# A three-part kernel on one Trainium2 core: score halves and transposes joined into shorter lists, loads and softmax moved ahead, tails' order written out

## The chip, the cores and the metric

The kernel runs on one core of a Trainium2 chip. The metric is the device time of one execution in microseconds; the median of three runs is given. The engines are TensorE (PE; its weight loads are PEld), VectorE (DVE), ScalarE (ACT), GpSimd (POOL) and SyncE (SP), which here issues loads and stores.

## The reference, cut

Three stages in a row, for 4 batches of 576 tokens: an attention over 32 memory slots made from `phi`, a mixture of experts with a sticky choice, and a gated convolution.

```python
a = softmax over seq of phi                       # (4, 8, 576, 32)
k_m, v_m = einsum('bhsm,bhsd->bhmd', a, k), ... v
attn = softmax(q @ k_m.T / sqrt(64)); x = attn @ v_m
logits = x @ w_gate; gate = sigmoid(x @ w_local)
e = argmax(logits[s]) if s == 0 or gate[s] < 0.5 else previous e
x[s] = p[e] * (relu(x[s] @ w1[e]) @ w2[e])
h = relu(x @ w_in); c = conv3(h, conv_w)
out = (h * sigmoid(c)) @ w_out
```

## The kernel before, in words

The work of a batch is two units (pairs of four heads), 2b and 2b+1. For a unit, `load_phi` and `load_kv` fetch it; `psoft` (`phi_softmax`: `phi_max` on VectorE writes `nm`, `phi_exp` on ScalarE writes `ex`, `phi_sums` on VectorE) makes A without its division; `pback` (`phi_back`, line 401) turns A on TensorE with five transposes into a PSUM tile `pa`, which ScalarE copies to `a`; `mem` (`memory`) multiplies A by k and v into `pk`, and its `memory_out` first lets VectorE use `pk` (`q0r`, line 452), then ScalarE scale it into `pm` (line 455). `back` (`memory_back`, line 459) turns both units' `pm` on TensorE into `pkt`, ScalarE copies that to `vt`.

For a batch, `scores` makes two halves of the scores on TensorE (`sc_0`, `sc_1`, a two-bank PSUM tile each, of a pool with two buffers). `strn` (`scores_back`, line 514) turns a half on VectorE into `st`; `smx`, `ssub`, `sexp`, `ssum` are the steps of its softmax (`mx`, `sd`, `smx`, `at`), and `ssoft` in the table at line 966 is all of them with `strn` ahead, through `slot_top` (line 557). `gatew` makes `pw`; `flog` (`first_expert`, line 601) makes the first token's logits `pfc` on TensorE, and their maximum `flm` and MAX_INDEX on VectorE, which writes `e0i`, the batch's expert. SP loads `e0i` and then, in one queue, the expert's weights (`w1`: `wa_0` to `wa_3`, `wb_0`, `wb_1`).

Then come the expert's products: `vw` folds the values into the first weights (`pv` on TensorE, its high part `vh` on ScalarE, its low part `vl` on VectorE). `h` (one of 16 for a batch, two halves of 8) is one `ph` of six matmuls in a single bank of a pool of four that also holds `pw`, `pfc`, `pk`, `pkt` and `py`; ScalarE writes its high part and VectorE its low part. `y` (8 for a batch) is one `py` of 24 matmuls. `nar` narrows the 64-bit words of the last stage's weights beside all this on ScalarE, VectorE and GpSimd.

TensorE runs in the order of a list. `OPENING` is written out, and `order` (lines 60 to 111) writes for each batch b its 24 slots (16 `h`, 8 `y`; batch 0 starts at slot 12) and what follows each: `FIRST` for batch 0, a table of its own for the others, with c = b + 1 and d = b + 2 the batches that are being prepared. VectorE's, ScalarE's and SP's instructions of the list are ordered by a scheduler, except in the opening and where an instruction is pinned (`keep_in_program_order`) or named to come after another (`issue_after`, `behind`, `behind_hidden`).

The last stage (`gated`, line 1048) makes, for f = 0 to 7, 12 matmuls `pi` for a batch's first 512 tokens, and for batch 0 also `pit`, the tails of all batches; ScalarE reads them out (`ht`, `htt`), the convolution and the gate follow, and `product` (line 1141) multiplies the result `g` by `w_out` into `po`, for batch 0 mixed between the `pit` by the scheduler.

Of the kernel before, what the change touches and what calls it, by code (L numbers as in the profile page):

```python
# [36 lines left out]
def units(b):  # L37
# [13 lines left out]


FIRST = {
    12: "gatew.1 scores.1.0 flog.1 w1.1 psoft.4", 13: "ssoft.1.0 psoft.5", 16: "pback.4 scores.1.1 ssoft.1.1", 17: "pback.5",
    19: "nar.2 nload.4", 20: "asplit.1.0 asplit.1.1",
    21: "mem.4 mem.5 vw.1.0 vw.1.1 vw.1.2 vw.1.3 back.2", 22: "w2.1.0 w2.1.1 nar.3 nload.5 conv", 23: "q.2.0 q.2.1 save.0",
}


def order():  # L60


    words = [4]

    def each(c, *parts):
        return [f"{part}.{u}" for u in units(c) for part in parts] if c < B else []

    def of(c, *parts):
        return [f"{part}.{c}" for part in parts] if c < B else []

    def narrow_next():
        i = words[0]
        words[0] += 1
        return [f"nar.{i}"] + [f"nload.{i + 2}"] * (i < 14)

    out = []
    for b in range(B):
        c, d = b + 1, b + 2
        whole = c < B
        after = {i: [] for i in range(24)}  # L80
        if b == 0:
            for i, more in FIRST.items():
                after[i] += more.split()
        else:
            for i, more in {
                1: [f"w2.{b}.2"] * (b == 2) + of(c, "frow", "fexp") + [f"save.{b}"],
                2: [f"w2.{b}.2"] * (b != 2) + of(d, "firstq") + each(d, "phi", "kv"),
                3: of(c, "gatew") + [f"rtok.{b // 2}"] * (b == 1) + [f"{item}.{c}.{hf}" for item in ("scores", "strn") for hf in range(2)] * whole
                   + of(c, "flog"),
                5: [f"smx.{c}.0"] * whole,  # L90
                6: [f"ssub.{c}.0", f"sexp.{c}.0"] * whole,
                7: [f"w2.{b}.3"],
                8: [f"ssum.{c}.0", f"smx.{c}.1", f"ssub.{c}.1", f"sexp.{c}.1", f"ssum.{c}.1"] * whole + each(d, "psoft"),
                9: of(c, "w1"),
                10: each(d, "pback"),
                12: [f"asplit.{c}.0", f"asplit.{c}.1"] * whole,
                21: each(d, "mem") + [f"vw.{c}.{q}" for q in range(4)] * whole + of(d, "back") + ["rtok.1"] * (b == 2),
                22: [f"w2.{c}.0", f"w2.{c}.1"] * whole,
                23: [f"q.{d}.0", f"q.{d}.1"] * (d < B),
            }.items():  # L100
                after[i] += more
            for i in ((), (6, 16, 18, 20, 22), (4, 7, 13, 15, 22, 22), (8, ))[b]:
                after[i] += narrow_next()
            if not whole:
                for i, more in {8: "rall rrows rpp", 9: "rown", 10: "close yload.0 win.0 win.1",
                                19: "ysplit.0", 20: "win.2 win.3"}.items():
                    after[i] += more.split()
        for i in range(0 if b else 12, 24):
            out += [f"h.{b}" if i % 12 < 8 else f"y.{b}"] + after[i]
    assert words[0] == 16  # L110
    return out
# [5 lines left out]
def fused_kernel(tc, q, first, first_q, kv, kv_tail, phi, w1, w2, w_in, conv_w, w_out, out):  # L117
# [3 lines left out]
    with (  # L121
# [116 lines left out]
        def behind(name):  # L238

            return tc.issue_after(issued[name]) if name else contextlib.nullcontext()  # L240

        def needed_behind(b):

            return None if b < 2 else f"wb{b - 2}_3"
# [124 lines left out]
        @contextlib.contextmanager  # L369
        def behind_hidden(wanted):  # L370

            with contextlib.ExitStack() as stack:
                if wanted:
                    stack.enter_context(urgent())
                    stack.enter_context(tc.issue_after(hidden_low[-1]))
                yield

        def phi_max(u):
            nms[u] = ap.tile([128, 1], F32, tag="nm", bufs=2, name=f"nm{u}")
            with behind_hidden(u >= 4):  # L380
                nc.vector.tensor_reduce(nms[u], phs[u], AX.X, ALU.max, negate=True)

        def phi_exp(u):
# [130 lines left out]
        def scores_back(b, hf):  # L514

            sts[b, hf] = work(f"st{b}_{hf}")
            nc.vector.transpose(two(sts[b, hf]), scs.pop((b, hf))[:, :, :HALF])

        def behind_h(b):
            return tc.issue_after(hidden_low[-1]) if b > 1 else contextlib.nullcontext()  # L520

        def slot_max(b, hf):
            mxs[b, hf] = ap.tile([128, 18], F32, tag="mx", bufs=2, name=f"mx{b}_{hf}")
# [30 lines left out]
                cols = slice(32 * hs.start, 32 * hs.stop)  # L554
                nc.vector.transpose(attf[b, hf].rearrange("p g t -> p (g t)")[:, cols], st[:, cols])

        def slot_top(b, hf):
            scores_back(b, hf)
            slot_max(b, hf)
            slot_difference(b, hf)  # L560

        def slot_softmax(b, hf):

            slot_top(b, hf)
            slot_exp(b, hf)
            slot_weights(b, hf)

# [361 lines left out]
        def split_tails(yp, nm):  # L929
            y, p = yp  # L930
            t = state.tile([128, 2, 4, B * TW], F32R, tag="ay", name=f"ts{nm}")
            parts = [t[:, i] for i in range(2)]
            if p is not None:
                nc.vector.tensor_tensor(y, y, p.rearrange("p (o s) -> p o s", o=1).to_broadcast([128, 4, B * TW]), ALU.mult)
            split(*parts, y)
            return parts
# [21 lines left out]
        def gated_w(kc):  # L958
# [4 lines left out]
            "phi": load_phi, "kv": load_kv, "q": load_q,  # L963
            "gates": load_gates, "psoft": phi_softmax, "pback": phi_back,
            "mem": memory, "memf": memory_out, "warm": warm, "back": memory_back,
            "scores": scores, "gatew": gate_weights, "firstq": first_queries, "frow": first_row, "fexp": first_weights, "flog": first_expert, "code": first_code, "ssoft": slot_softmax,
            "pmax": phi_max, "pexp": phi_exp, "prec": phi_sums, "smax": slot_top, "strn": scores_back, "smx": slot_max,
            "ssub": slot_difference, "sexp": slot_exp, "ssum": slot_weights, "ahi": attention_high, "alo": attention_low,
            "rtok": route_tokens, "save": save, "rrows": route_rows, "rall": route_all, "rpp": route_scan, "rown": route_first, "asplit": split_attention,
            "vwe": first_vw, "vwh": first_vw_high, "vwl": first_vw_low, "vw": expert_vw, "w2": expert_w2, "nload": load_words, "nar": narrow, "win": gated_w,  # L970
# [77 lines left out]
        def gated(gp, nm, scaled=False):  # L1048
# [23 lines left out]
            def columns(name, y, store, pin=lambda ins: ins, between=lambda f: None):  # L1072

                yh, yl = y
                n = yh.shape[-1]
                before = None
                for f in range(8):
                    fs = slice(f * 128, (f + 1) * 128)
                    ps = pairs[-1].tile([128, 512], F32, tag="pi", bufs=1 if scaled else 4, name=f"pi{name}_{f}")[:, :n]
                    matmul3([(ps, slice(0, n))],  # L1080
                            [((wi[kc][:, 0, fs], wi[kc][:, 1, fs]), (yh[:, kc, :], yl[:, kc, :])) for kc in range(4)], pin)
                    finish = gate(*before, store) if before else lambda: None
                    ht = lp.tile([128, S], F32, tag="cv", name=f"ht{name}_{f}")[:, :n]
# [23 lines left out]
            for b in range(B):  # L1107
# [17 lines left out]
                    while len(wo) < 4 and f >= WO[len(wo)]:  # L1125
                        wo.append(w2_piece(f"wo{len(wo)}", slow(f"wo.{len(wo)}")))

                columns(f"{nm}{b}", ys, store_main, tc.keep_in_program_order if b == 0 else lambda ins: ins, between)
                if b == 0:
                    tails = split_tails(tails, nm)  # L1130
                    yn = load_y(1, first(1))
                    columns(f"{nm}t", tails, store_tail)
                    for f in range(8):
                        close_main(f)
                if b + 1 < B:
                    ys = y_parts(b + 1)
                    split_y(b + 1, yn, *ys)

                pin = tc.keep_in_program_order if b == B - 1 else lambda ins: ins

                def product(ps, c, fr):
                    for f in fr:
# [5 lines left out]
                                                                    start=f == 0 and i == 0, stop=f == 7 and i == 2)).ins]  # L1148

                chunks = [0, 1, 2] + [4] * (b % 2) + [3]  # L1150
                pss = {c: bank(f"po{b}_{c}") for c in chunks[:3]}
                for c in chunks[:3]:
                    product(pss[c], c, range(0, 6))
                for c in chunks:
                    if c in pss:
                        product(pss[c], c, range(6, 8))
# [96 lines left out]
```

## Time and profile before

| | |
|---|---|
| median of 3 runs | 406.47 us (405.45, 406.47, 406.55) |
| the profiled execution | 405.78 us in all, its span 403.9 us |
| TensorE clock granted | 1.00 over the span |
| busy: DVE, ACT, POOL | 283.4 us (70%), 228.1 us (56%), 65.2 us (16%) |
| busy share of the DMA engines, 40 to 60 us and 60 to 80 us | 0.94, 1.02 |

A timeline row gives when an instruction, or a row of equal ones, started, how long it (or the row) took, the engine, the line, the operation and the count. A matmul's end is modelled, so starts are compared with starts. A row such as `x16` for eight matmuls stands for the two passes of each in full fp32. The share of DMA may go a little over 1 in a short stretch.

### The profile page before, as it was taken

The page shows a single profiled execution, that of the slowest core. Times are in us where ns is not written, and L with a number is a line of the kernel's source. Part 1 is how long each engine was busy: PE and PEld are TensorE (multiplying, and loading weights), DVE is VectorE, ACT ScalarE, POOL GpSimd, SP SyncE. Part 2 cuts the span into 40 slices and gives each one's busy share as a digit, 9 for nine tenths or more (in the row PEclk, how much of TensorE's full clock was granted, in tenths as well). Part 3 has the DMA queues.
Part 4 walks back from the last instruction along what each step waited for, and adds up shares of the span by engine and source line. Part 5 has one row for each costly group of instructions (what it writes and reads, how often), then busy time and mean ns, then how long its engine had stood idle before and what let it go on. Part 6 is the DMA issues. An engine that isn't in the chain of part 4 may idle for free. (4 is left out here: it accounts for less than half of the span.)

```text
span 403.9 us, 7760 instructions
## 1 busy us (share of the span) xinstructions
PE 397.2 (98%) x2969; PEld 344.0 (85%) x2970; DVE 283.4 (70%) x545; ACT 228.1 (56%) x457; POOL 65.2 (16%) x128
## 2 busy tenths in 40 slices
PE   7999999999999999999999999999999999999996
PEld 3469998899989998999988888888888888888884
DVE  3689898897689986696868999489601895069500
ACT  4466575565476357465767758468321882268311
POOL 1000201402112211310100314304100041002200
PEclk9999999999999999999999999999999999999999
DMA  7999989999476959945313033200021000200022
GB/s 274 337 382 407 377 274 393 409 404 368 106 265 211 386 127 409 384 148 181 108 54 109 26 105 104 104 2 2 2 78 52 2 0 0 106 0 0 3 80 57
DMA packets 26525, 69.03 MB, mean 171 GB/s; under 512 B 5904, under 2 KB 6672, under 8 KB 26480
## 3 DMA queue, kind: packets, MB, share of 16 engines
q1 hardware_dynamic: 22896, 56.92, 39.5%
q0 software_dynamic: 3584, 11.54, 7.3%
q8 instruction: 25, 0.41, 0.4%
q14 instruction: 20, 0.16, 0.1%
HBM read 52.12 MB, written 16.33 MB: 169 GB/s over the span
## 5 line engine op out<-in xcount | busy, mean ns | idle before, releaser
L166 PE MATMUL py<-h,wb 128*128 128x288 f32 x768 | 104.5, 295 | 0.0
L166 PEld LDWEIGHTS py<-h,wb 128*128 128x128 f32 x768 | 102.4, 188 | 0.4 <-issue 0.3
L1147 PE MATMUL po<-wo,g 128*128 128x512 f32 x360 | 82.9, 389 | 0.0
L166 PE MATMUL pi<-yh,wi 128*128 128x512 f32 x256 | 79.5, 389 | 0.0
L1147 PEld LDWEIGHTS po<-wo,g 128*128 128x128 f32 x360 | 67.4, 188 | 14.0
L166 PEld LDWEIGHTS pi<-yh,wi 128*128 128x128 f32 x256 | 48.1, 188 | 10.0
L1068 DVE SCALAR_TENSOR_TENSOR ct<-ht,convw,ct 128x510 f32<-128x510 f32 x32 | 23.9, 747 | 45.6 <-ACT ct L1066 45.6
L166 PE MATMUL ph<-att,vh 128*128 128x288 f32 x256 | 52.6, 299 | 0.0
L166 PE MATMUL pi<-yl,wi 128*128 128x512 f32 x128 | 49.8, 389 | 0.0
L166 PEld LDWEIGHTS ph<-att,vh 128*128 128x128 f32 x256 | 40.7, 188 | 2.6 <-issue 0.9
L894 POOL DMA_DIRECT2D ydram<-ys x32 | 17.8, 556 | 146.2 <-ACT ys L893 142.8
L166 PE MATMUL ph<-att,vl 128*128 128x288 f32 x128 | 37.7, 296 | 0.0
L809 ACT ACTIVATE h<-ph 128x288 fp32r<-128x288 f32 x64 | 25.5, 409 | 18.6 <-PE ph L166 18.5
L810 DVE SCALAR_TENSOR_TENSOR h<-ph,h 128x288 fp32r<-128x288 f32 x64 | 27.8, 449 | 8.6 <-ACT h L809 8.3
L1173 ACT ACTIVATE ot<-po 128x512 f32<-128x512 f32 x17 | 9.9, 597 | 41.4 <-PE po L1147 41.4
L154 POOL TENSOR_TENSOR g<-ct,g 128x511 fp32r<-128x511 f32 x12 | 16.3, 1362 | 104.9 <-ACT g L153 104.9
L893 ACT ACTIVATE ys<-py 128x288 f32<-128x288 f32 x32 | 13.0, 407 | 34.3 <-PE py L166 16.1
L1069 DVE SCALAR_TENSOR_TENSOR ct<-ht,convw,ct 128x511 f32<-128x511 f32 x32 | 30.4, 951 | 0.5
L1085 ACT ACTIVATE ht<-pi 128x512 f32<-128x512 f32 x32 | 19.0, 594 | 20.5 <-PE pi L166 20.5
L166 PEld LDWEIGHTS pi<-yl,wi 128*128 128x128 f32 x128 | 24.0, 188 | 4.9
L153 ACT ACTIVATE g<-ct 128x511 fp32r<-128x511 f32 x32 | 19.7, 625 | 13.7 <-DVE ct L1099 13.3
L1099 DVE TENSOR_TENSOR ct<-ht,ct 128x511 f32<-128x511 f32 x32 | 23.5, 735 | 5.3 <-ACT ct L1098 5.0
(250 smaller groups left out, 556.7 us busy)
## 6 DMA issues: line engine op xcount, KB each, us to landing
q<-in_q SPq DMA_DIRECT2D x8, 576.0 KB, 9.0
ydram<-ys POOLq DMA_DIRECT2D x32, 144.0 KB, 5.1
kv<-in_kv SPq DMA_DIRECT2D x8, 512.0 KB, 7.5
kv<-in_kv SPq DMA_DIRECT2D x4, 1024.0 KB, 10.5
y<-ydram SPq DMA_DIRECT2D x4, 1024.0 KB, 5.8
out<-ot SPq DMA_DIRECT2D x15, 256.0 KB, 2.0
ph<-in_phi SPq DMA_DIRECT2D x8, 288.0 KB, 7.0
adram<-at POOLq DMA_DIRECT2D x8, 288.0 KB, 6.7
```

The lines of the kernel that those rows point to most:

```text
L153: pin(nc.scalar.activation(hi, src, AF.Copy))
L154: pin((eng or nc.vector).tensor_tensor(lo, src, hi.bitcast(F32), ALU.subtract))
L166: pin(nc.tensor.matmul(ps, st, mv[:, cols], start=i == 0, stop=i == len(terms) - 1))
L809: nc.scalar.activation(t[:, 0, :], ps, AF.Relu)
L810: low = nc.vector.scalar_tensor_tensor(t[:, 1, :], ps, 0.0, t[:, 0, :].bitcast(F32), ALU.max, ALU.subtract)
L893: nc.scalar.activation(yt, ps, AF.Copy)
L894: stored.append(nc.gpsimd.dma_start(ydram[b, d, :, half(hf)], yt).ins)
L1068: nc.vector.scalar_tensor_tensor(ct[..., a:], ht[..., :n - a], w(0), ct[..., a:], ALU.mult, ALU.add)
L1069: nc.vector.scalar_tensor_tensor(ct[..., :more], ht[..., first + 1:first + 1 + more], w(2), ct[..., :more], ALU.mult, ALU.add)
L1085: nc.scalar.activation(ht, ps, AF.Relu)
L1099: slow(f"gm.{f}").tensor_tensor(ct, own, ct, ALU.mult)
L1147: last_product[:] = [pin(nc.tensor.matmul(ps, st[sp], w[:, mp, f % 2, :], start=f == 0 and i == 0, stop=f == 7 and i == 2)).ins]
```

## The change

It changes the list and the last stage's order; no operation is added or left out in what is executed.

- Batch 0's list (`FIRST`): both halves of the scores and both their transposes on VectorE stand in slot 12, ahead of `flog`; the softmax of a half is `soft` without `strn`. `pback.4` and `pback.5` stand together in slot 17. The loads `phi.6` and `phi.7` go to slot 13, `psoft.6` and `psoft.7` to slot 23.
- The list of the others: `pback` of d's units (in batch 1: units 6 and 7) goes from slot 10 into slot 3, ahead of `gatew`; `phi` and `psoft` leave it.
- `load_phi` of units 6 and 7 follows the load `wb1_1`; `phi_max` is named behind a hidden product for units 4 and 5 alone; `behind_h` holds from batch 1 on.
- In the last stage the products of batch 0 that stand between the `pit` are written out (8 of an f after the third `pit`, 5 after the sixth), pinned, and the first six f of the three first chunks of every batch come in the order of `ahead_of`.

```diff
-    12: "gatew.1 scores.1.0 flog.1 w1.1 psoft.4", 13: "ssoft.1.0 psoft.5", 16: "pback.4 scores.1.1 ssoft.1.1", 17: "pback.5",
+    12: "gatew.1 scores.1.0 strn.1.0 scores.1.1 strn.1.1 flog.1 w1.1 psoft.4", 13: "soft.1.0 psoft.5 phi.6 phi.7",
+    16: "soft.1.1", 17: "pback.4 pback.5",
...
-    21: "mem.4 mem.5 vw.1.0 vw.1.1 vw.1.2 vw.1.3 back.2", 22: "w2.1.0 w2.1.1 nar.3 nload.5 conv", 23: "q.2.0 q.2.1 save.0",
+    21: "mem.4 mem.5 vw.1.0 vw.1.1 vw.1.2 vw.1.3 back.2", 22: "w2.1.0 w2.1.1 nar.3 nload.5 conv", 23: "q.2.0 q.2.1 save.0 psoft.6 psoft.7",
...
-                2: [f"w2.{b}.2"] * (b != 2) + of(d, "firstq") + each(d, "phi", "kv"),
-                3: of(c, "gatew") + [f"rtok.{b // 2}"] * (b == 1) + [f"{item}.{c}.{hf}" for item in ("scores", "strn") for hf in range(2)] * whole
+                2: [f"w2.{b}.2"] * (b != 2) + of(d, "firstq") + each(d, "kv"),
+                3: each(d, "pback") + of(c, "gatew") + [f"rtok.{b // 2}"] * (b == 1) + [f"{item}.{c}.{hf}" for item in ("scores", "strn") for hf in range(2)] * whole
...
-                8: [f"ssum.{c}.0", f"smx.{c}.1", f"ssub.{c}.1", f"sexp.{c}.1", f"ssum.{c}.1"] * whole + each(d, "psoft"),
+                8: [f"ssum.{c}.0", f"smx.{c}.1", f"ssub.{c}.1", f"sexp.{c}.1", f"ssum.{c}.1"] * whole,
                 9: of(c, "w1"),
-                10: each(d, "pback"),
...
-            with behind(needed_behind(u // 2)):
+            with behind("wb1_1" if u >= 6 else needed_behind(u // 2)):
                 nc.sync.dma_start(phs[u], phi[u])
...
-            with behind_hidden(u >= 4):
+            with behind_hidden(u in (4, 5)):
                 nc.vector.tensor_reduce(nms[u], phs[u], AX.X, ALU.max, negate=True)
...
-            return tc.issue_after(hidden_low[-1]) if b > 1 else contextlib.nullcontext()
+            return tc.issue_after(hidden_low[-1]) if b > 0 else contextlib.nullcontext()
...
-        def slot_top(b, hf):
-            scores_back(b, hf)
+        def slot_softmax(b, hf):
...
+                pin = tc.keep_in_program_order if b in (0, B - 1) else lambda ins: ins
...
+                ahead_of = [(c, f) for cs, fs in (((0, 1), range(4)), ((2,), range(4)), ((0, 1, 2), (4, )), ((0, 1, 2), (5, )))
+                            for c in cs for f in fs]
...
-                    columns(f"{nm}t", tails, store_tail)
+                    columns(f"{nm}t", tails, store_tail, pin, lambda f: products_ahead({2: 8, 5: 5}.get(f, 0)))
...
-                for c in chunks[:3]:
-                    product(pss[c], c, range(0, 6))
+                products_ahead(len(ahead_of))
```

VectorE's order in batch 0's slots 12 to 14, before (a number in a name is the half or the slot; the last is the buffer's):

```order
L517 STREAM_TRANSPOSE st_0_845<-sc_0_795 128x576
L608 MAX flm_807<-pfc_804 1x8
L389 TENSOR_SCALAR rs_829<-rs_829 128x1
L810 SCALAR_TENSOR_TENSOR h_11_842<-ph_11_835,h_11_842 128x288
L381 TENSOR_REDUCE nm_857<-ph_620 128x1
L609 MAX_INDEX e0i<-flm_807,pfc_804 1x8
L390 RECIPROCAL rs_829<-rs_829 128x1
L525 TENSOR_REDUCE mx_0_847<-st_0_845 128x18
```

and after:

```order
L517 STREAM_TRANSPOSE st_0_804<-sc_0_795 128x576
L517 STREAM_TRANSPOSE st_1_815<-sc_1_806 128x576
L604 MAX flm_820<-pfc_817 1x8
L389 TENSOR_SCALAR rs_842<-rs_842 128x1
L806 SCALAR_TENSOR_TENSOR h_11_855<-ph_11_848,h_11_855 128x288
L381 TENSOR_REDUCE nm_868<-ph_620 128x1
L525 TENSOR_REDUCE mx_0_858<-st_0_804 128x18
L605 MAX_INDEX e0i<-flm_820,pfc_817 1x8
```

`st_1` now stands ahead of `flm`, and `mx_0` ahead of MAX_INDEX.

VectorE's order in batch 0's slots 21 to 23, after (`nm` is that of units 6 and 7, `q0r` that of units 4 and 5):

```order
L555 STREAM_TRANSPOSE at_1_919<-st_1_815 128x576
L381 TENSOR_REDUCE nm_1223<-ph_877 128x1
L452 SCALAR_TENSOR_TENSOR q0r_618,first_95<-pk_1040,rs_846,q0r_618 128x64
L381 TENSOR_REDUCE nm_1232<-ph_879 128x1
L723 TENSOR_TENSOR att_1007<-at_1_919,att_1007 128x2x288
L452 SCALAR_TENSOR_TENSOR q0r_618,first_95<-pk_1057,rs_875,q0r_618 128x64
```

Before, both `q0r` follow `at_1` directly, then `att`; both `nm` stood in batch 1's stage. On ScalarE the two `ex` of units 6 and 7 stand one ahead of each `pm`.

SP's queue behind the weights of batch 1's expert, after:

```order
L294 DMA wb_1r<-in_w 128x1024
L345 DMA ph_877<-in_phi 128x576
L345 DMA ph_879<-in_phi 128x576
L365 DMA q_0_1216<-in_q 128x1152
L365 DMA q_1_1218<-in_q 128x1152
```

The two `ph` stood further back, behind `wb_2r`, `wb_3r` and `q0r`, with a `kv` between them.

## Rows read from the trace of the kernel before

**Rows 1.** The page, part 1: busy us (share of span) xinstructions of each engine.
```profile
PE 397.2 (98%) x2969; PEld 344.0 (85%) x2970; DVE 283.4 (70%) x545; ACT 228.1 (56%) x457; POOL 65.2 (16%) x128
```

**Rows 2.** Timeline of TensorE, batch 0's second half: start us, us, line, operation, count.
```profile
48.30 0.29 PE L166 MATMUL ph<-att,vl 128*128 128x288 f32 x1
...
49.53 0.54 PE L166 MATMUL ph<-att,vh 128*128 128x288 f32 x2
...
52.06 0.53 PE L166 MATMUL ph<-att,vh 128*128 128x288 f32 x2
...
52.83 0.29 PE L166 MATMUL ph<-att,vl 128*128 128x288 f32 x1
...
54.24 0.53 PE L166 MATMUL ph<-att,vh 128*128 128x288 f32 x2
...
55.01 0.29 PE L166 MATMUL ph<-att,vl 128*128 128x288 f32 x1
...
55.61 0.51 PE L166 MATMUL ph<-att,vh 128*128 128x288 f32 x2
```

**Rows 3.** Timeline of TensorE, the same small operations alone, at three places.
```profile
29.16 0.29 PE L166 MATMUL ph<-att,vl 128*128 128x288 f32 x1
...
30.03 0.53 PE L166 MATMUL ph<-att,vh 128*128 128x288 f32 x2
...
92.62 0.82 PE L166 MATMUL py<-h,wb 128*128 128x288 f32 x5
93.28 0.60 PE L407 MATMUL pa<-ident,ex 128*128 128x128 f32 x4
...
94.29 0.38 PE L166 MATMUL py<-h,wb 128*128 128x288 f32 x1
...
124.37 0.29 PE L166 MATMUL ph<-att,vl 128*128 128x288 f32 x1
...
126.08 0.40 PE L166 MATMUL ph<-att,vh 128*128 128x288 f32 x1
```

**Rows 4.** Timeline of VectorE from 49.5 us on, the argmax of batch 1.
```profile
49.51 0.74 DVE L381 TENSOR_REDUCE nm<-ph 128x1 f32<-128x576 f32 x1
...
50.76 0.78 DVE L517 STREAM_TRANSPOSE st<-sc 128x576 f32<-128x576 f32 x1
51.46 0.12 DVE L608 MAX8 flm<-pfc 1x8 f32<-1x8 f32 x1
...
51.56 0.43 DVE L810 SCALAR_TENSOR_TENSOR h<-ph,h 128x288 fp32r<-128x288 f32 x1
...
52.66 0.15 DVE L609 FIND_INDEX8 e0i<-flm,pfc 1x8 uint32<-1x8 f32 x1
...
52.80 0.72 DVE L525 TENSOR_REDUCE mx<-st 128x18 f32<-128x576 f32 x1
```

**Rows 5.** SP's timeline, its loads (KB, us to landing), and busy by stretch with GB/s.
```profile
53.73 0.35 SPq L288 DMA_DIRECT2D wa_0r<-in_w  x1
...
56.95 1.09 SPq L294 DMA_DIRECT2D wb_1r<-in_w  x1
...
wb_1r<-in_w SPq DMA_DIRECT2D x1, 512.0 KB, 8.4
...
66.00:68.00 2.00, 2.00 (x72) 1.15 (x64) 1.27 (x5) 1.21 (x6) 0.00 (x0) 1.00 1.02 381
```

**Rows 6.** Timelines of VectorE, ScalarE and TensorE at `pm` and `pkt`.
```profile
66.27 0.28 DVE L452 SCALAR_TENSOR_TENSOR q0r<-pk,rs,q0r 128x64 f32<-128x64 f32 x1 [0.61 <-PE pk L429]
...
66.48 0.76 DVE L727 TENSOR_TENSOR att<-at,att 128x576 fp32r<-128x576 f32 x1
...
66.11 0.85 ACT L455 ACTIVATE pm<-pk,rs 128x128 f32<-128x128 f32 x2
...
68.02 0.44 PE L464 MATMUL pkt<-ident,pm 128*128 128x128 f32 x2
```

**Rows 7.** Tile `htt` (us, times): who waited for it.
```profile
  PEld pit L166: 0.3, 1
```

More of the change, by code (lines that the diff above doesn't have):

```diff
@@ L555, in slot_weights @@
                 nc.vector.transpose(attf[b, hf].rearrange("p g t -> p (g t)")[:, cols], st[:, cols])
-        def slot_top(b, hf):
-            scores_back(b, hf)
+        def slot_softmax(b, hf):
             slot_max(b, hf)
             slot_difference(b, hf)
-        def slot_softmax(b, hf):
-            slot_top(b, hf)
             slot_exp(b, hf)
@@ L965, in fused_kernel @@
             "mem": memory, "memf": memory_out, "warm": warm, "back": memory_back,
-            "scores": scores, "gatew": gate_weights, "firstq": first_queries, "frow": first_row, "fexp": first_weights, "flog": first_expert, "code": first_code, "ssoft": slot_softmax,
-            "pmax": phi_max, "pexp": phi_exp, "prec": phi_sums, "smax": slot_top, "strn": scores_back, "smx": slot_max,
+            "scores": scores, "gatew": gate_weights, "firstq": first_queries, "frow": first_row, "fexp": first_weights, "flog": first_expert, "code": first_code, "soft": slot_softmax,
+            "pmax": phi_max, "pexp": phi_exp, "prec": phi_sums, "strn": scores_back, "smx": slot_max,
             "ssub": slot_difference, "sexp": slot_exp, "ssum": slot_weights, "ahi": attention_high, "alo": attention_low,
@@ L1126, in between @@
                         wo.append(w2_piece(f"wo{len(wo)}", slow(f"wo.{len(wo)}")))
[L1128 to L1131, printed above, removed]
-                    columns(f"{nm}t", tails, store_tail)
[L1133 to L1139, printed above, removed]
+                pin = tc.keep_in_program_order if b in (0, B - 1) else lambda ins: ins
                 def product(ps, c, fr):
@@ L1150, in gated, with products_ahead @@
                 chunks = [0, 1, 2] + [4] * (b % 2) + [3]
-                pss = {c: bank(f"po{b}_{c}") for c in chunks[:3]}
-                for c in chunks[:3]:
-                    product(pss[c], c, range(0, 6))
+                pss = {}
+                def products_ahead(n):
+                    for _ in range(n):
+                        c, f = ahead_of.pop(0)
+                        if c not in pss:
+                            pss[c] = bank(f"po{b}_{c}")
+                        product(pss[c], c, [f])
+                ahead_of = [(c, f) for cs, fs in (((0, 1), range(4)), ((2,), range(4)), ((0, 1, 2), (4, )), ((0, 1, 2), (5, )))
+                            for c in cs for f in fs]
+                columns(f"{nm}{b}", ys, store_main, tc.keep_in_program_order if b == 0 else lambda ins: ins, between)
+                if b == 0:
+                    tails = split_tails(tails, nm)
+                    yn = load_y(1, first(1))
+                    columns(f"{nm}t", tails, store_tail, pin, lambda f: products_ahead({2: 8, 5: 5}.get(f, 0)))
+                    for f in range(8):
+                        close_main(f)
+                if b + 1 < B:
+                    ys = y_parts(b + 1)
+                    split_y(b + 1, yn, *ys)
+                products_ahead(len(ahead_of))
                 for c in chunks:
```

## The prediction

> **What bounds the kernel.** I read the page first. TensorE is busy 98% of the span [rows 1], so a stage gets shorter only where TensorE's own chain gets shorter, and longer wherever TensorE is made to wait. Then I read TensorE's timeline around the second half of batch 0 (starts 48.30 to 55.61 us) and at three other places where the same small operations stand alone [rows 2, 3], VectorE's timeline of the same stretch [rows 4], SP's queue with the landing of its loads [rows 5], and the chain from the A products to `pkt` [rows 6], where TensorE has little left: the two `pm` are done at 66.96 (66.11 and 0.85), 1.06 us ahead of `pkt`. One row tells of a wait in the tails' stage [rows 7].
>
> **The joined runs, batch 0.** Before, three runs of small operations cut the stream of `ph` matmuls; a run's price is from the last `ph` start before it to the first after it. `pw`, one half of the scores and `pfc`: 48.30 to 49.53, 1.23 us. Unit 4's transposes with the other half: 52.83 to 54.24, 1.41. Unit 5's transposes: 55.01 to 55.61, 0.60 [rows 2]. Together 3.24. After, two runs: `pw`, both halves, `pfc`, as batch 2's stage has them, 124.37 to 126.08, 1.71; and ten transposes, whose five preceding `py` start 0.13 apart (92.62 to 93.28), the last at 93.15, with the stream back at 94.29: 1.14 [rows 3]. Together 2.85: TensorE saves 0.39 us.
>
> **The moved transposes (units 6, 7).** Their run of 1.14 us goes, and ten transposes of 0.10 each (1.01 from 93.28 to 94.29) are added ahead of `pw` in the next logits' run. What does joining unlike operations save? Unit 4's transposes joined with a score half cost 1.41. Alone, a score half costs 0.87 (29.16 to 30.03) and five transposes 0.60; less one ordinary interval of 0.13 that both hold, 1.34 [rows 2, 3]. So that join saved nothing, and I take 0, between 0 and 0.13 (1.14 less 1.01). The Trainium skill (TensorEngine Tiling (Array Packing), Key Properties) says that changing the tiling mode drains TensorE. By it each removed run would save its drain, whatever it is joined with, this part would give its 0.13, and the sum would be +2.4; the row of 1.41 speaks against that here.
>
> **VectorE behind the joined scores.** After, both score transposes `st_0`, `st_1` stand ahead of the maximum `flm`, and the reduction `mx_0` ahead of MAX_INDEX. A transpose holds VectorE 0.70 us (50.76 to 51.46); `mx_0` takes 0.72, some 0.65 beyond overlap [rows 4]. Two things follow.
> First, MAX_INDEX, which ended at 52.81 (52.66 and 0.15), ends 1.35 later, at 54.16. It frees the bank of `pfc` that the built program hands to `ph_15`, before as after. `ph_11` to `ph_14` are pushed 0.48 by the second score half (1.71 less 1.23). `ph_14`, at 52.06, would come at 52.54; it also waits for `h_11`'s low part on VectorE, 0.70 later than 51.56 with 0.43 of work [rows 4], so 52.7 to 52.8: 0.2 lost. Taking 0.9 as before (52.06 to 52.83 and 0.13), it leaves TensorE free at 53.65, and `ph_15` starts near 54.25: 0.6 lost. After `ph_15` (0.9) and the ten transposes, `ph_16` starts at 54.25 + 0.9 - 0.13 + 1.14 = 56.15 instead of 55.61 [rows 2]. So the two waits outweigh the saving, and TensorE is 0.55 us late.
> Second, the expert's number reaches SP 1.35 later, and so do all loads that hang on it. `wa_0r` was issued at 53.73, the first of six loads of 512 KB in SP's queue; the last, `wb_1r`, was issued at 56.95 and landed 8.4 later, at 65.35 [rows 5].
>
> **The moved loads and softmax.** `phi.6` and `phi.7` (288 KB each) now stand in SP's queue right behind `wb_1r`, which lands at 65.35 + 1.35 = 66.7. The queues moved 381 GB/s at 66 to 68 us [rows 5], so 0.29 MB takes 0.77 us: unit 6 lands near 67.5, unit 7 near 68.3. `psoft.6` and `.7` sit in batch 0's last slot, and VectorE's order is now `at_1`, `nm` of 6, `q0r` of 4, `nm` of 7, `att`, `q0r` of 5. VectorE takes them in this order, so `q0r`, which needs no phi, stands behind a load. ScalarE's second `pm` needs that `q0r`, and `pkt` needs that `pm`. The chain: unit 6 at 67.5; `nm` 0.74 less overlap, 68.2 [rows 4]; `q0r` of 4, 0.2 (66.27 to 66.48) [rows 6], 68.4; `nm` of 7, 69.1; `att` 0.76 less overlap, 69.8; `q0r` of 5, 0.28, 70.1 (now the second `pm` may start). The pair of `pm` took 0.85 for two, so one some 0.4: 70.55. `pkt`, at 68.02 before [rows 6], would be reached at 68.02 + 0.55 = 68.57; it waits 2.0 us and stands at +2.5.
> Bounds. If both loads were there in time, `pkt` would keep its 0.55. If unit 6 took the 8.4 of `wb_1r` from an issue 1.2 behind it (56.95 + 1.35 + 1.2 = 59.5), it would land at 67.9, and `pkt` would stand at +2.9. I take +2.5, the queue's own order and rate. What lies later on ScalarE and VectorE (`vh`, `vl`, the splits of `wb`) moves by some 3 us; the first `ph` of batch 1 comes two whole `py` products (48 matmuls at 0.13, 6.3 us) behind `pkt`, which covers that. I count nothing.
>
> **Tails.** The same matmuls in another order, all of one shape. TensorE lost 0.3 us to one wait of `pit` for ScalarE [rows 7]. The block of products ahead of it grows from 22 matmuls to 24, which covers it; the next block shrinks from 18 to 15, which uncovers as much of the same kind of wait for the last `pit`. Net 0; at most the 0.3 is won, or as much is lost again.
>
> **Sum.** +2.5 with the joins already in it, 0 for units 6 and 7's run, 0 for the tails. The profiled execution took 405.8 us in all (span 403.9), 0.7 below the median of the three runs shown, 406.5. 405.8 + 2.5 = 408.3; from the median 409.0. I write 408.6, the middle.
>
> **Rivals.**
> *The loads are early enough (not slower).* The point that decides is the landing of unit 6: the chain from it to `pkt` is 3.05 us, so at 65.5 or before `pkt` waits for nothing and only the bank's wait is left, +0.55, or with the tails' 0.3 won +0.2: 406.0 to 407.0. For it: the two loads are small. Against it: six large loads go out ahead, and the last took 8.4 us to land, about what all six take one behind the other (six of 0.52 MB at 381 GB/s: 8.3 us). The Trainium skill (DMA: Bandwidth & Descriptors, Queues, rings and completion order) says that completion is not first-in first-out per issuing engine. By that rule a late small load may be complete before an early large one, which would be this rival; the 8.4 of the last load speaks for order here. 15%.
> *The runs' savings alone.* No new wait reaches TensorE: 0.39, 0.13 and 0.3 won, -0.8, 405.0 to 405.7. It needs a MAX_INDEX that is not late, against [rows 4]. 10%.
> *More is late.* The lateness of 3 us on ScalarE and VectorE runs into batch 1's first `ph`, or the late expert's weights into a product: another 1 to 2 us, 409.5 to 410.5. 7%.
>
> **How the numbers follow.** Forecast 68%. About 0.3%, 1.2 us, is what a measurement can tell from no change. The forecast lies 2.1 us over the median; with `pkt` at its lower bounds some 5 of its 68 points end inside 1.2. Slower: 63 and 7 = 0.70. Same: 5, 15 and 5 of the runs' rival = 0.25. Faster: the other 5 = 0.05. The range goes from 406.0, the low end of the first rival, to 410.0: it leaves out the runs' rival and the upper half of the last, with a few points of the rest.
>
> **What would show it.** Right: `ph_15` starts 0.5 us or more after the matmul ahead of it could let it; `nm` of units 6 and 7 wait for DMA on VectorE at 66 to 68; `pkt` waits for `pm` 1.5 to 2.5 us; the first `wa_0r` of batch 1 is issued near 55.1. Wrong: `pkt` near 68.6 or earlier, `nm` without a wait, or TensorE's start in batch 1 less than 1 us later than now.

## The result and the profile after

The changed kernel is slower: 409.36 us (median of 8 runs, 408.86 to 411.62) beside 406.46 (8 runs of the kernel before, 405.35 to 407.67), ratio 1.0092 with a 95% interval of 1.0074 to 1.0109. A second set of four runs (410.11 to 411.73) gave 1.0118 (1.0100 to 1.0136). The runs form two groups: five of the twelve have a mean granted clock of 1.000 (408.86 to 409.61 us), seven have 0.996 (410.11 to 411.73); the profiled execution, 410.49 us with a span of 408.7, is of the second group.

The page's first part hardly moves; it answers to [rows 1]. TensorE's work is the same, so its busy time should be too:

```profile
PE 399.1 (98%) x2969; PEld 346.2 (85%) x2970; DVE 283.7 (69%) x545; ACT 228.0 (56%) x457; POOL 64.8 (16%) x128
```

1.9 us more busy for the same 2969 matmuls is a first sign that some of them ran slower.

TensorE's timeline of batch 0's second half (start us, us, engine, line, operation, count, and in brackets the idle time ahead and what ended it), the answer to [rows 2]:

```profile
48.49 0.29 PE L166 MATMUL ph<-att,vl 128*128 128x288 f32 x1
...
50.21 0.53 PE L166 MATMUL ph<-att,vh 128*128 128x288 f32 x2
...
52.57 0.29 PE L166 MATMUL ph<-att,vl 128*128 128x288 f32 x1
52.91 0.53 PE L166 MATMUL ph<-att,vh 128*128 128x288 f32 x2
...
53.68 0.29 PE L166 MATMUL ph<-att,vl 128*128 128x288 f32 x1
54.38 0.53 PE L166 MATMUL ph<-att,vh 128*128 128x288 f32 x2 [0.41 <-DVE rs L390]
...
55.14 0.30 PE L166 MATMUL ph<-att,vl 128*128 128x288 f32 x1
...
56.29 0.52 PE L166 MATMUL ph<-att,vh 128*128 128x288 f32 x2
```

The two joined runs cost 1.72 (48.49 to 50.21) and 1.15 (55.14 to 56.29) in place of 1.23, 1.41 and 0.60: 0.37 won. The starts 52.57 to 52.91 and 53.68 to 54.38, ordinarily 0.13 apart, hold 0.21 and 0.57 of waiting. They follow VectorE, which has the low part of `h_11` at 52.42, against 51.56 in [rows 4], and MAX_INDEX (FIND_INDEX8) at 54.17, against 52.66:

```profile
52.32 0.12 DVE L604 MAX8 flm<-pfc 1x8 f32<-1x8 f32 x1
...
52.42 0.43 DVE L806 SCALAR_TENSOR_TENSOR h<-ph,h 128x288 fp32r<-128x288 f32 x1
...
53.45 0.73 DVE L525 TENSOR_REDUCE mx<-st 128x18 f32<-128x576 f32 x1
...
54.17 0.15 DVE L605 FIND_INDEX8 e0i<-flm,pfc 1x8 uint32<-1x8 f32 x1
...
68.01 0.75 DVE L381 TENSOR_REDUCE nm<-ph 128x1 f32<-128x576 f32 x1 [2.33 <-DMA ph<-in_phi]
68.68 0.27 DVE L452 SCALAR_TENSOR_TENSOR q0r<-pk,rs,q0r 128x64 f32<-128x64 f32 x1
...
68.88 0.75 DVE L381 TENSOR_REDUCE nm<-ph 128x1 f32<-128x576 f32 x1
69.54 0.75 DVE L723 TENSOR_TENSOR att<-at,att 128x576 fp32r<-128x576 f32 x1
70.21 0.28 DVE L452 SCALAR_TENSOR_TENSOR q0r<-pk,rs,q0r 128x64 f32<-128x64 f32 x1
```

The last five rows are the chain that the prediction wrote: `nm` of unit 6 waits 2.33 us for its load, and `q0r` stands behind it. SP's rows (the last is the time to landing) say when that load left, where [rows 5] had `wa_0r` at 53.73:

```profile
54.87 0.35 SPq L288 DMA_DIRECT2D wa_0r<-in_w  x1
...
58.64 1.54 SPq L345 DMA_DIRECT2D ph<-in_phi  x2
...
ph<-in_phi SPq DMA_DIRECT2D x2, 288.0 KB, 9.2
```

On ScalarE and TensorE the chain goes on to `pkt`, at 68.02 in [rows 6]; the last row is the 48 `py` behind it:

```profile
68.85 0.78 ACT L386 ACTIVATE ex<-ph,nm 128x576 f32<-128x576 f32 x1 [2.45 <-DVE nm L381]
...
69.62 0.35 ACT L455 ACTIVATE pm<-pk,rs 128x128 f32<-128x128 f32 x1
69.87 0.76 ACT L386 ACTIVATE ex<-ph,nm 128x576 f32<-128x576 f32 x1
...
70.63 0.35 ACT L455 ACTIVATE pm<-pk,rs 128x128 f32<-128x128 f32 x1
...
71.03 0.54 PE L464 MATMUL pkt<-ident,pm 128*128 128x128 f32 x2 [2.23 <-ACT pm L455]
71.22 8.16 PE L166 MATMUL py<-h,wb 128*128 128x288 f32 x48
```

`pkt` waits 2.23 us. What comes behind it was not foreseen. Busy time by stretch (the stretch in us and its length; PE, PEld, DVE, ACT, POOL, each with its count; then the granted clock, DMA share, GB/s); four rows of the change, and one of the kernel before:

```profile
68.00:70.00 2.00, 0.80 (x32) 0.28 (x16) 1.99 (x5) 1.15 (x4) 0.00 (x0) 1.00 1.01 381
70.00:72.00 2.00, 0.97 (x5) 0.97 (x6) 1.37 (x12) 2.00 (x6) 0.00 (x0) 0.81 1.04 415
72.00:74.00 2.00, 2.00 (x10) 2.00 (x9) 1.90 (x6) 2.00 (x5) 0.00 (x0) 0.50 1.03 418
74.00:76.00 2.00, 2.00 (x14) 2.00 (x14) 2.00 (x2) 2.00 (x4) 0.00 (x0) 0.84 1.03 401
...
72.00:74.00 2.00, 2.00 (x18) 2.00 (x17) 2.00 (x5) 1.68 (x6) 0.03 (x1) 1.00 1.05 404
```

From 72 to 74 us the granted clock is 0.50, the lower of its two levels (1.2 GHz), and TensorE starts 10 matmuls there; in the kernel before the same stretch had 18 at clock 1.00. The `py` behind `pkt` start 0.24 us apart instead of 0.13, and the 48 take 8.16 us, where they took 6.59 before. Of the fourteen profiles of this case only this one and the change's second have such a fall before the last matmul has started.

Whole times scatter by more than these steps: the last `ph` ahead of batch 0's `pw`, up to which all kernels here do the same, starts at 48.16 to 49.71 us in the profiles. So I read each profile from that start on, by TensorE's starts: the *passage* to the last `py` ahead of `pk`; the `pk` *run* to the first `py` behind `pkt`; the stream behind it (*`py` behind*: the 48 `py` and the `ph` after them) up to the next run; and batch 1's *run* of `pw`, `pl`, `sc`, `pfc`, with or without units 6 and 7's transposes (where they are in it, their own run of 1.14 us is missing later).

| kernel | passage | `pk` run | `py` behind | batch 1's run | start of passage to the last matmul |
|---|---|---|---|---|---|
| before | 15.21 | 4.71 | 9.46 | 2.81 | 351.50 |
| change | 15.72 | 7.01 | 11.03 | 3.91 | 356.11 |
| change, second profile | 15.73 | 7.11 | 11.00 | 3.91 | 356.04 |
| without units 6, 7's part | 15.71 | 4.70 | 9.49 | 2.82 | 352.04 |
| units 6, 7's part alone | 15.21 | 6.88 | 9.49 | 3.91 | 353.46 |
| index first | 14.73 | 6.74 | 9.46 | 3.91 | 353.19 |
| index first, `pm` first | 14.73 | 5.91 | 9.46 | 3.91 | 352.04 |
| `nm` in batch 1 | 15.72 | 4.70 | 9.49 | 6.05 | 354.20 |
| index first, no units 6, 7's part | 14.73 | 4.71 | 9.46 | 2.81 | 351.03 |
| index first, `nm` behind `vl` | 14.73 | 4.71 | 9.46 | 3.91 | 351.25 |
| fillers | 15.73 | 7.48 | 9.49 | 3.91 | 355.40 |

For the change: +0.51 in the passage, +2.30 at `pkt`, +1.57 in the slow `py`, -0.04 by the join in batch 1 (3.91 against 2.81 and 1.14), and +0.27 at `pkt` of the next batch, seen in the first profile alone: 4.61 together.

### The profile page after: what moved, and what is told of

Read it like the earlier page. It is cut to its first block, busy times and chain, and to the rows that moved or that the text cites. A ratio compares the mean times of both kernels' runs of the same rounds, so it can differ in the third digit from the quotient of the medians.

```text
span 408.7 us, 7761 instructions
## 1 busy us (share of the span) xinstructions
PE 399.1 (98%) x2969; PEld 346.2 (85%) x2970; DVE 283.7 (69%) x545; ACT 228.0 (56%) x457; POOL 64.8 (16%) x128
## 5 line engine op out<-in xcount | busy, mean ns | idle before, releaser
L166 PE MATMUL py<-h,wb 128*128 128x288 f32 x768 | 105.9, 298 | 0.0
L166 PEld LDWEIGHTS py<-h,wb 128*128 128x128 f32 x768 | 104.0, 191 | 0.5 <-issue 0.3
```

The source lines that it names most:

```text
L166: pin(nc.tensor.matmul(ps, st, mv[:, cols], start=i == 0, stop=i == len(terms) - 1))
```

## The experiments

**1. Units 6 and 7 as before.** Their loads, softmax and transposes go back to their old places.

```diff
-    12: "gatew.1 scores.1.0 strn.1.0 scores.1.1 strn.1.1 flog.1 w1.1 psoft.4", 13: "soft.1.0 psoft.5 phi.6 phi.7",
+    12: "gatew.1 scores.1.0 strn.1.0 scores.1.1 strn.1.1 flog.1 w1.1 psoft.4", 13: "soft.1.0 psoft.5",
...
-                2: [f"w2.{b}.2"] * (b != 2) + of(d, "firstq") + each(d, "kv"),
+                2: [f"w2.{b}.2"] * (b != 2) + of(d, "firstq") + each(d, "phi", "kv"),
...
+                10: each(d, "pback"),
...
-            with behind("wb1_1" if u >= 6 else needed_behind(u // 2)):
+            with behind(needed_behind(u // 2)):
...
-            with behind_hidden(u in (4, 5)):
+            with behind_hidden(u >= 4):
```

> The changed kernel with its part on units 6 and 7 taken back (their loads, softmax and transposes stand where they stood before); the joined score halves, the joined transposes and the tails' order stay. Theory: the loss is `pkt` of batch 2 waiting behind the maxima nm6 and nm7 on VectorE, so that wait of 2.2 us is gone (under 0.2 us), no stretch of the batch 0 to batch 1 passage falls to 1.2 GHz, and what is left is the runs' saving (-0.4) and the two bank waits at ph_14 and ph_15 behind the late MAX_INDEX (0.2 + 0.6): 406.5 to 407.3 us, ratio 1.000 to 1.002. Rival (the loss is the joined scores' and tails' own): 408.5 to 409.5 us, ratio 1.005 to 1.0075.

Measured: 407.10 us (12 runs), ratio 1.0015 (1.0006 to 1.0025), as the theory had it. `pkt` has no wait, and no run has a clock below 0.999. The passage still holds the two bank waits. So by the ratios five sixths of the loss hang on units 6 and 7.

**2. Units 6 and 7's part alone,** on the kernel before.

```diff
-    12: "gatew.1 scores.1.0 flog.1 w1.1 psoft.4", 13: "ssoft.1.0 psoft.5", 16: "pback.4 scores.1.1 ssoft.1.1", 17: "pback.5",
+    12: "gatew.1 scores.1.0 flog.1 w1.1 psoft.4", 13: "ssoft.1.0 psoft.5 phi.6 phi.7", 16: "pback.4 scores.1.1 ssoft.1.1", 17: "pback.5",
...
-                10: each(d, "pback"),
...
-            with behind(needed_behind(u // 2)):
+            with behind("wb1_1" if u >= 6 else needed_behind(u // 2)):
```

> The kernel before with only the part on units 6 and 7 (loads behind the second weight row of batch 1, softmax at the end of batch 0, transposes in batch 1's run). MAX_INDEX is on time, so SP's loads go out as before. Theory (nm6 and nm7 on VectorE hold up `pkt`): phi.6 and phi.7 land near 66.5 and 67.3, `pkt` still waits, 1.0 to 1.8 us, and the time is 407.5 to 408.5 us, ratio 1.0025 to 1.005. Rival (the late expert index alone made the loads late): no wait of `pkt` over 0.3 us, 406.2 to 406.8 us, ratio 0.999 to 1.001.

Measured: 409.88 us (6 runs), ratio 1.0093 (1.0068 to 1.0119): as large a loss as the whole change, above what I expected. With MAX_INDEX on time VectorE waited 1.81 us for the load and `pkt` 2.11 for `pm`:

```profile
68.01 0.75 DVE L380 TENSOR_REDUCE nm<-ph 128x1 f32<-128x576 f32 x1 [1.81 <-DMA ph<-in_phi]
...
71.61 0.44 PE L463 MATMUL pkt<-ident,pm 128*128 128x128 f32 x2 [2.11 <-ACT pm L454]
```

The late index is not what makes `pkt` wait. In this profile, of the second shortest run, the loss from the start of the passage to the last matmul is 1.96 us (353.46 against 351.50); what makes the ratio of the whole times larger was not traced. Here the `py` behind are at full speed (9.49); four of the six runs have a clock of 0.992 to 0.996.

**3. MAX_INDEX first.** The second half's transposition on VectorE is issued after it.

```diff
-    12: "gatew.1 scores.1.0 strn.1.0 scores.1.1 strn.1.1 flog.1 w1.1 psoft.4", 13: "soft.1.0 psoft.5 phi.6 phi.7",
+    12: "gatew.1 scores.1.0 strn.1.0 scores.1.1 flog.1 strn.1.1 w1.1 psoft.4", 13: "soft.1.0 psoft.5 phi.6 phi.7",
...
+            with tc.issue_after(indexed[1]) if (b, hf) == (1, 1) else contextlib.nullcontext():
+                nc.vector.transpose(two(sts[b, hf]), scs.pop((b, hf))[:, :, :HALF])
```

(`indexed[1]` is batch 1's MAX_INDEX.)

> The changed kernel with one edge added: the transposition of the second score half on VectorE is issued after MAX_INDEX of batch 1, so MAX_INDEX stands before it and before mx_0 as in the kernel before. Theory: the waits at ph_14 and ph_15 are gone (0.8 us in sum), the weights of batch 1 are issued near 53.7 again, phi.6 and phi.7 land some 1.1 us earlier (66.9 and 67.6), and `pkt` waits 1.0 to 1.4 us less than the 2.2 of the change: 406.8 to 407.8 us, ratio 1.001 to 1.0035. Rival (the late index is the whole loss): no wait of `pkt`, 405.8 to 406.3 us. Rival (lateness is made good in `pkt`'s wait whatever its source, so the loads land as late): 408.5 to 409.3 us.

Measured: 409.40 us (6 runs), ratio 1.0091 (1.0071 to 1.0112), against 406.8 to 407.8 by the theory. Both bank waits are gone: the passage is 14.73, 0.48 under the kernel before. The low part of `h_11` is even later here (53.15), and `ph_14` starts ahead of it (53.11); so `ph_14` seems to have another bank in this build, as the one that MAX_INDEX frees is free earlier (52.45). And the loads came over 2 us earlier (`nm` waited 0.19 us), against the rival that they land as late, yet `pkt` waited nearly as long. VectorE, ScalarE and TensorE, in this order:

```profile
65.66 0.75 DVE L381 TENSOR_REDUCE nm<-ph 128x1 f32<-128x576 f32 x1 [0.19 <-DMA ph<-in_phi]
...
68.53 0.28 DVE L452 SCALAR_TENSOR_TENSOR q0r<-pk,rs,q0r 128x64 f32<-128x64 f32 x1
...
68.60 0.35 ACT L455 ACTIVATE pm<-pk,rs 128x128 f32<-128x128 f32 x1
68.85 1.01 ACT L775 ACTIVATE vh<-pv 128x1024 fp32r<-128x1024 f32 x1
69.75 0.37 ACT L455 ACTIVATE pm<-pk,rs 128x128 f32<-128x128 f32 x1
...
70.17 0.44 PE L464 MATMUL pkt<-ident,pm 128*128 128x128 f32 x2 [1.96 <-ACT pm L455]
```

Two `nm`, both `ex` and, by the scheduler's new order, one `vh` and on VectorE a second `att` (66.33, between the two `nm`) stand ahead of the second `pm`. The theory that the landing of the loads sets the size was wrong here: what stands in the queues ahead of `pm` is enough.

**4. The same, with `vh` behind the second `pm` on ScalarE.**

```diff
+            with tc.issue_after(pm_done[-1]) if len(pm_done) == 6 else contextlib.nullcontext():
+                highs.append(nc.scalar.activation(hi[:, fs], ps.rearrange("p g (f n) -> p f g n", f=4)[:, fs], AF.Copy).ins)
```

(`pm_done` holds the `pm` so far; the sixth is unit 5's.)

> The changed kernel with MAX_INDEX on time and, on ScalarE, the high parts vh of batch 1 issued after the second `pm` of batch 2; nm and ex of units 6 and 7 stay ahead of `pm`. In the run with the index alone on time phi.6 landed at 65.63 and VectorE's q0r of unit 5 ended at 68.8, but a vh of 0.9 us stood between the two pm, and `pkt` waited 1.96 us. Theory (lateness of the loads and places in the queues both count): `pkt` waits 0.9 to 1.3 us, batch 0's passage keeps its 0.5 us of saving, 406.6 to 407.4 us where the clock stays up. Rival (the loads' lateness counts for nothing, the queues for all): `pkt` still waits 1.8 us or more. Rival (vh was all that was left): `pkt` waits under 0.4 us.

Measured: 407.69 us (4 runs, all at clock 1.000), ratio 1.0041 (1.0026 to 1.0055). The wait is 1.13, in the forecast span, so one `vh` was worth 0.83 of it; the whole time is 0.3 over the expected one.

```profile
65.49 0.75 DVE L381 TENSOR_REDUCE nm<-ph 128x1 f32<-128x576 f32 x1 [0.25 <-DMA ph<-in_phi]
...
68.43 0.62 ACT L455 ACTIVATE pm<-pk,rs 128x128 f32<-128x128 f32 x2
...
69.10 0.44 PE L464 MATMUL pkt<-ident,pm 128*128 128x128 f32 x2 [1.13 <-ACT pm L455]
```

`nm` waited 0.25 us for its load, so of the 1.13 at least 0.88 is the price of places in the queues. This doesn't split the change's 2.23 into late loads and places: VectorE has another order here, with a second `att` ahead of both `q0r`, which the change has earlier (63.65).

**5. The softmax of units 6 and 7 in batch 1,** behind its second hidden product (`h`) and out of batch 0's last slot; loads as late as in the change.

```diff
...
-                1: [f"w2.{b}.2"] * (b == 2) + of(c, "frow", "fexp") + [f"save.{b}"],
+                1: each(d, "psoft") + [f"w2.{b}.2"] * (b == 2) + of(c, "frow", "fexp") + [f"save.{b}"],
...
-            with behind_hidden(u in (4, 5)):
+            with behind_hidden(u >= 4):
```

> The changed kernel with the softmax of units 6 and 7 issued in batch 1's second step, behind its second hidden product, instead of at the end of batch 0; their loads stay as late as in the change, and MAX_INDEX too. Theory (the order on VectorE is what delays `pkt`, not the loads as such): `pkt` waits under 0.3 us, ph_14 and ph_15 still wait 0.2 and 0.6, and nm6 and nm7 (0.7 us each) now stand between two hidden products of batch 1, where four banks cover them or cost up to 0.8: 406.6 to 407.6 us, ratio 1.0005 to 1.003. Rival (the joined scores bunch VectorE's work, so att and q0r are late without nm6 and nm7): `pkt` waits 1.5 us or more, 408.3 us or more.

Measured: 409.53 us (6 runs), ratio 1.0088 (1.0072 to 1.0104), against my 406.6 to 407.6. `pkt` indeed waits no longer, though the loads are late. But the transposes of units 6 and 7, the thing that the change moved up, now wait for `ex`:

```profile
69.06 0.44 PE L464 MATMUL pkt<-ident,pm 128*128 128x128 f32 x2
...
78.31 1.40 DVE L381 TENSOR_REDUCE nm<-ph 128x1 f32<-128x576 f32 x2
...
79.83 0.77 ACT L386 ACTIVATE ex<-ph,nm 128x576 f32<-128x576 f32 x1
...
80.75 0.66 PE L407 MATMUL pa<-ident,ex 128*128 128x128 f32 x4 [1.71 <-ACT ex L386]
```

I had priced `nm` between two hidden products and not asked what reads `ex` next. The wait had only changed its place, with batch 1's run at 6.05.

**6. Index first, and `nm` of units 6 and 7 behind the second `vl`.**

```diff
-            with behind_hidden(u in (4, 5)):
+            with tc.issue_after(lows[-1]) if u >= 6 else behind_hidden(u in (4, 5)):
```

(`lows` holds the `vl` so far.)

> The changed kernel with MAX_INDEX on time (as in the run with the index first) and the maxima of units 6 and 7 issued on VectorE after the second vl of batch 1, so behind all that `pkt` needs and 4 us before the transposes of these units. Theory (the price of the part on units 6 and 7 is only where nm and ex stand on VectorE and ScalarE): neither `pkt` nor pa waits over 0.3 us, the run of transposes, gate, logits and scores in batch 1 takes 3.9 us in place of 2.8 + 1.1 in two runs, and the time is that of the change without this part and with the index first, within 0.5 us: 405.8 to 406.9 us. Rival (3 us of work on VectorE and ScalarE have no free place before batch 1's run, since something of batch 1 waits wherever they stand): 407.5 us or more, with a new wait of 1 us or more at wb, h or ph.

Measured: 405.79 us (12 runs), ratio 0.9993 (0.9980 to 1.0007). There is a free place: `nm` at 70.59, `ex` at 72.58 and 73.63, and neither `pkt` nor `pa` waits.

```profile
70.59 1.40 DVE L381 TENSOR_REDUCE nm<-ph 128x1 f32<-128x576 f32 x2
...
72.58 0.79 ACT L386 ACTIVATE ex<-ph,nm 128x576 f32<-128x576 f32 x1
```

**7. Index first, without units 6 and 7's part.** The edits of 1 and 3 together.

> The changed kernel without its part on units 6 and 7, and with the transposition of the second score half on VectorE issued after MAX_INDEX of batch 1: what is left of the change are the joined score halves, the joined transposes and the tails' order. Theory: beside the run without the part on units 6 and 7 (407.1 us, bank waits of 0.21 and 0.57 at ph_14 and ph_15) those two waits are gone and the joined runs keep their 0.4: 405.8 to 406.4 us, ratio 0.9985 to 1.000. Rival (the bank waits come from the order of the matmuls and not from MAX_INDEX): 406.8 to 407.3 us, ratio 1.001 to 1.002.

Measured: 405.73 us (12 runs), ratio 1.0000 (0.9987 to 1.0013): at the edge of the theory's span, with the bank waits gone. Beside 6 it shows what the moved transposes are worth once nobody waits: nothing that the runs can tell, and 0.04 us in the stage table.

**8. The tails' order alone,** on the kernel before (the last stage's lines of the change, nothing else).

> The kernel before with only the tails' order written out. Theory: nothing, within 0.3 us: ratio 0.999 to 1.001; the one 0.3 us wait of pit at 236.8 us goes or becomes smaller. Rival (the tails' order is part of the loss): 407 us or more, ratio 1.0015 or more.

Measured: 406.57 us (11 runs), ratio 1.0014 (1.0001 to 1.0027), at the edge between the two. From the start of the passage to the last matmul its profile has 351.38 us against 351.50. Experiments 9 and 10, which take the tails' order away, have the ratios of 7 and 6 again, so the runs show no price of it.

**9. Joins and index alone,** with the tails' order of before.

> The kernel before with only the joined score halves and joined transposes of batch 0, and MAX_INDEX on time (the transposition of the second score half issued after it); units 6 and 7 and the tails as before. Theory: from the start of `pw` of batch 0 to the last py ahead of pk of batch 2 TensorE takes 14.73 us in place of 15.21, and the whole 405.4 to 406.1 us beside 406.1 to 406.4 of before, ratio 0.998 to 0.9995. Rival (the tails' order carried part of the gain in the runs that had both): 406.1 us or more, ratio 1.000 or more.

Measured: 406.01 us (12 runs), ratio 1.0001 (0.9986 to 1.0017). The passage is 14.74 as forecast, but the ratio lies above the expected span: a gain in whole time is not shown. From the start of the passage to the last matmul its profile has 350.75 us, 0.75 under the kernel before: 0.47 of it in the passage, while the last stage, in the same order, was 0.32 shorter in this execution.

**10. As 6, with the tails' order of before.**

> The changed kernel with MAX_INDEX on time and the maxima of units 6 and 7 after the second vl of batch 1, but with the tails' order of before. Theory: as with the tails' order, within 0.3 us (the order of the tails is worth nothing): 405.4 to 406.1 us, ratio 0.998 to 0.9995, and the same time as the joins alone within 0.4 us, since joining these transposes to the logits' run saves 0.04 us. Rival (the tails' order costs 0.4 us, as its run alone could mean): 0.3 to 0.5 us faster than with it, 405.2 us or so.

Measured: 405.86 us (12 runs), ratio 0.9992 (0.9981 to 1.0004), as with it. 6 and 10 have the lowest ratios of all, and neither interval excludes 1: no version here is shown to be faster than the kernel before.

**11. Fillers.** Three matmuls that nobody reads are added ahead of `pkt`; they compute nothing of the reference.

```diff
-    21: "mem.4 mem.5 vw.1.0 vw.1.1 vw.1.2 vw.1.3 back.2", 22: "w2.1.0 w2.1.1 nar.3 nload.5 conv", 23: "q.2.0 q.2.1 save.0 psoft.6 psoft.7",
+    21: "mem.4 mem.5 vw.1.0 vw.1.1 vw.1.2 vw.1.3 warm.9.9 back.2", 22: "w2.1.0 w2.1.1 nar.3 nload.5 conv", 23: "q.2.0 q.2.1 save.0 psoft.6 psoft.7",
```

> The changed kernel with three matmuls of the identity added (two float32, one float32r, into a bank of their own, read by nobody) between the last pv and `pkt` of batch 2, where TensorE stands idle for 2.2 us. Theory (the granted clock falls because TensorE has just been idle): `pkt` starts as late as in the change, but no run has a mean granted clock below 0.998, no stretch near 70 to 76 us is at 1.2 GHz, and the median is 408.6 to 409.4 us with no run over 410. Rival (the fall has nothing to do with this idle stretch): three or so of eight runs still at 0.996 and 410.4 us or more. If the fillers are longer than the wait, up to 0.5 us more in both.

Measured: 409.29 us (6 runs, 407.74 to 410.69), ratio 1.0074 (1.0055 to 1.0093). `pkt` comes as late (its `pk` run is 7.48), but no run has a clock below 0.998, and the `py` behind take 9.49, as before. Two of the six runs lie over 410 at clock 1.000 (410.20 and 410.69); this part of the expectation failed. TensorE, then the stretch that was at 0.50:

```profile
69.63 1.98 PE L482 MATMUL idle<-ident 128*128 128x512 f32 x4
71.05 0.80 PE L482 MATMUL idle<-ident_r 128*128 128x512 f32 x1
72.41 0.44 PE L464 MATMUL pkt<-ident,pm 128*128 128x128 f32 x2 [0.56 <-ACT pm L455]
...
72.00:74.00 2.00, 1.59 (x12) 1.60 (x13) 1.36 (x8) 2.00 (x7) 0.00 (x0) 1.00 1.02 410
```

**12. The change once more,** unedited.

> The changed kernel itself, for a second profile and more runs beside the others on one chip. Theory: the same 2.2 us wait of `pkt`, the same waits at ph_14 and ph_15; where the mean granted clock is 1.000 the py behind `pkt` start 0.13 us apart and the time is 408.7 to 409.6 us, where it is 0.996 they start 0.24 apart for some 3 us and the time is 1.5 us longer. Rival (the longer runs wait longer for `pkt`, and the clock only goes along): in a profile at 1.000 the wait of `pkt` is 1 us or more shorter.

Measured: 411.07 us (4 runs, all at clock 0.996), ratio 1.0118 (1.0100 to 1.0136). The profile repeats the first: `pkt` waits 2.33, then the clock falls.

```profile
71.76 0.44 PE L464 MATMUL pkt<-ident,pm 128*128 128x128 f32 x2 [2.33 <-ACT pm L455]
...
72.00:74.00 2.00, 2.00 (x11) 2.00 (x10) 1.37 (x4) 2.00 (x5) 0.00 (x0) 0.52 1.00 407
```

No run of this set was at 1.000, so whether the runs of the change at 1.000 wait as long stays open: none of them was profiled. Experiment 3's profile, of the shortest of its six runs, has a wait of 1.96 us without a fall.

## Why the prediction was right or wrong

The sign was right, and so was the chain; the size was too small. 406.46 times 1.0092 is 410.2 us, beyond the range's upper end of 410.0 and 1.6 over the forecast of 408.6. The median of the eight runs, 409.36, is 0.8 over the forecast and inside the range; the runs at the lower clock, 410.1 to 411.7, are all outside. By the prediction's own steps:

- *Joined runs, batch 0.* Forecast -0.39, with 2.85 for the two; measured 2.87, -0.37. Without the waits the passage wins 0.48, in part since the third matmul behind each run starts 0.38 us after the first (49.53 to 49.91 before) and not 0.26, now twice and not three times.
- *Bank waits.* Forecast 0.2 and 0.6, TensorE 0.55 late; measured 0.21 and 0.57, and 0.51 late. Experiment 3 shows the cause: with the second transposition of the scores behind MAX_INDEX on VectorE, both are gone; that `ph_14` doesn't meet `h_11`'s low part there was not foreseen, and it rests on the banks of that build.
- *Moved transposes.* Forecast 0; measured -0.04. Joining unlike operations saves next to nothing, as the row of 1.41 had said. The Trainium skill (TensorEngine Tiling (Array Packing), Key Properties) has a change of tiling mode drain TensorE; this trace shows at most 0.04 us for a run less.
- *Loads and `pkt`.* Forecast a wait of 2.0, measured 2.23 and 2.33. Unit 6's load landed at 67.98 and not 67.5; as the passage starts 0.19 later in this profile, that is inside the bounds given (67.9). From there every row came as written, 0.5 later. But the reason was half right. The prediction let the landing of the loads decide, and gave 15% to the case that they are early enough. They were early in experiments 3 and 4 (landed at 65.63 and 65.47, next to the 65.5 named as the point), and `pkt` waited 1.96 and 1.13 all the same; by the prediction's chain of 3.05 us from the landing it would have been 0.5 and 0.6 there. What lengthened the chain was the order, `att` and `vh` in experiment 3 and `att` in 4.
- *Tails.* Forecast 0, and nothing else is shown. The tile `htt` lists no wait of TensorE in the first profile of the change, where [rows 7] had 0.3, but that is no effect of the order: the wait is 0.3 again in the change's second profile and 0.4 in experiment 6, and it is absent from experiments 9 and 10, which have the order of before. From the first `pi` to the last matmul the stage took 196.7 to 197.0 us in the four profiles with the order of before and 196.8 to 197.4 in the ten with the written one; if the order costs anything, it is some 0.3.
- *Sum.* **The step that failed** is "I count nothing" for what follows `pkt`. It was written of ScalarE and VectorE, and there it held. But TensorE itself, just left idle for 2 us, went on at a granted clock of 0.50 (1.2 GHz): 1.57 and 1.54 us in the two profiles of the change (`py` behind: 11.03 and 11.00 against 9.46). No term of the sum and no rival had that. In runs at clock 1.000 the change costs 2.5 us by their median (408.97), which is the forecast's +2.5, though none of them was profiled; in those at 0.996, 4.6 (411.04). The last rival, "more is late", reached 410.5, but through another mechanism.

What supports idleness as the cause of the fall, short of showing it: the fall comes right behind the wait in both profiles; with the idle stretch filled no run of six has a clock below 0.998, and `pkt` is no earlier in the one that was profiled; and of the kernels with a wait of some 2 us 18 of 30 runs are at 0.996 or less (change 7 of 12, experiments 2, 3 and 5 4, 4 and 3 of 6), of those without any (1 and 6 to 10) 7 of 71. Those 7, and a few runs of the kernel before, at 0.992 to 0.996 show that the clock falls in other places too; their place was not traced, nor was that of the fall in the low runs of experiments 2, 3 and 5. The fillers ran on a third chip, without the change itself beside them, so a difference of the chips is not excluded there; on each of the two others kernels with and without the wait did run side by side (11 of 18 low runs against 0 of 12, and 4 of 4 against 3 of 24).

## What to carry to other kernels

A step moved earlier in a list moves ahead of something on every engine that it uses: write down, queue by queue, what now stands behind it and who reads that, since a load that lands in time does not make the move free. Here a place behind the second `vl` (`nm` at 70.59, where experiment 3 had 65.66) cost nothing, and the run it was moved for was worth 0.04 us. Where a forecast leaves TensorE idle, price the stretch behind the wait as well, at both clock levels. Where a step is smaller than the scatter of whole runs, measure it in the trace between two starts of TensorE.

## What the runs showed of the hardware

Behind an idle stretch of TensorE of 2.23 us, matmuls 0.24 apart cost another 1.57 us. By the mean granted clock (0.996 in 7 of 12 runs, 1.000 in 5) this comes in some executions of a program and not in others; an execution of the change without it was not profiled. The Trainium skill (TensorE: Matmul & The Clock Gate, Part 1: The HAM clock gate) says of this clock that the default state is throttled and activity releases it; the granted clock of 0.50 behind the wait, and 1.00 in the same place with fillers, agree.

One instruction's place on an engine that is far from full can cost most of its own time: one `vh` of 1.01 us ahead of `pm` was worth 0.83 us (1.96 against 1.13), and ScalarE is busy 56% of the span.
